# Retention, top-1 experts and a gated channel mix in one kernel: where the second half of wv is narrowed, which engine weighs the rows, and where the first constants stand

## The chip, the cores and the metric

The kernel runs on one core of one Trainium2 chip. The metric is device time in microseconds (us) of one execution; a kernel's time is the median of its runs. Engines are named as in the profile: PE is TensorE, DVE VectorE, ACT ScalarE, POOL GpSimd, SP SyncE, which issues most DMAs. PEld stands for TensorE's weight loads.

## The reference, cut to what matters

Three blocks follow one another, for 2 sequences of 768 tokens and 512 features. The weights of the third block, w_k, w_v and w_r, arrive in double precision; the rest is f32.

```python
# 1 retention, 8 heads of 64, in blocks of 64 tokens
intra = einsum(qb, kb) * Dmask @ vb
inter = (qb * lam_pow) @ kv_state
out = intra + inter
kv_state = lam_block * kv_state + einsum(kb * rev_pow, vb)
# 2 top-1 experts: one of 8 per token (a token can keep its predecessor's)
h = max(x[b, s] @ w1[e], 0)          # w1[e]: 512 x 1024
out[b, s] = p[e] * (h @ w2[e])       # w2[e]: 1024 x 512
# 3 channel mix
xk = mu_k * x + (1 - mu_k) * x_prev
xr = mu_r * x + (1 - mu_r) * x_prev
k = max(xk @ w_k, 0)                 # 512 x 1024
v = k * k @ w_v                      # 1024 x 512
r = sigmoid(xr @ w_r)                # 512 x 512
return r * v
```

## The kernel before, in words

The order of instructions on every engine is written out by hand: what the code issues first, the engine has first in its queue.

**First stage (to about 85 us).** Retention and routing in 12 units of 128 tokens (a pair of units, one per sequence, makes a chunk). `load_qk(u)` and `load_kv(u)` are SyncE's loads of 512 KB each; the two `kv` loads of a chunk fill one tile, and two such tiles exist. `iot`, which holds index patterns, takes the place of one of them until `constants()` (L244) has read it. `scores(u)` (L262) makes the product of q and k on TensorE and multiplies it with the mask on VectorE (`stm`, L281); with the second unit of a chunk it scales k for the state on ScalarE (`kd`, L267). `values(u)` (L284) makes output and state, `gate(u)` the gate's logits. `constants()` is called after the first unit's scores: four scans from `lamp` into `tab` and eight small operations on VectorE.

**Experts (about 85 to 280 us).** Each product is made of three, of high and low parts in fp32r: high x high, high x low, low x high (`split3`, L649). A weight comes in pieces of 128 x 1024 f32: `w_load` (L139) has SyncE load one into one of four `raw` buffers, `w_split` (L147) makes the high part on ScalarE (L158) and the low part on VectorE (L159), then loads the piece four further on. Per expert there are `up` (four times: eight products, then `hh` on ScalarE, L666, and `hl` on VectorE, L667), `flip` of the next expert's inputs (L646, `xsTh`, `xsTl`), and `down` for two halves of 128 tokens, whose results (`y`, L713) GpSimd scatters to `Y_n`. At four points of `up` and four of `down` the function `side_w` (L972) is called; I number its 64 calls 0 to 63, so that expert e has calls 8e to 8e + 7, the first four in `up`. In each call it divides a weight piece and takes a step of a generator:

- `narrow()` (L751), called `conv`: narrows wk, wr and the first half of wv from double precision to f32, part by part (128 x 512). A part has three steps, each with two VectorE operations (`narrow_1` L740 and L741, `narrow_2` L744 and L745, `narrow_3` L748 and L749). The third step also queues the DMA that writes the part to DRAM (`written`, issued at the next call), issues the next part's `magnitude` on ScalarE (L736), and has SyncE read the part after that into one of two `raw64` buffers. What is written is loaded again later as ordinary weight pieces, which wait for the writes. Parts 0 to 15; the last is written out at call 52.
- `direct()` (L788), called `tail`, from call 56: the four pieces of the second half of wv. Each is loaded in double precision into a `raw` buffer by `w_load`, narrowed in the same six VectorE operations, and divided at once into high and low parts (L803, L808). Two pieces fall into expert 7, two into the channel mix, between `r_part(0)` and `v_part(0)`.

w_v's high and low parts stand where those of expert 6's w2 were, so they can be written only after expert 6.

**Passage.** While expert 7 runs its `down`, the first 256 tokens are prepared for the channel mix: VectorE weighs rows that are already back from DRAM (`xg_`, L888) and the expert's own results (`weighed`, L907, `yll`); TensorE moves both into `ps_f` (`others` L902, `own` L920); `mix_first` mixes them.

**Channel mix (about 280 us to the end).** Six groups n of 256 tokens. `read(n)` fetches rows from `Y_n`, `weigh(n)` (L1026) multiplies the two halves by the gate's probability, one on VectorE (L1033), one on ScalarE (L1031); `fetch(n)` (L1038) transposes on TensorE (L1051) and copies on ScalarE (L1052); `mix(n, i)` makes the inputs of w_k (i = 0) and w_r (i = 1) on ScalarE (L941, L953) and VectorE (L945, L954). `k_part(n)` makes four steps of 24 products with `rl` and Square on ScalarE, `sq` and `k2l` on VectorE (L1105, L1106). `r_part(n)` and `v_part(n)` make the rest; VectorE multiplies both into `o` (L1134). In the steady loop the order is `v_part(n-1)`, with `weigh(n+1)`, `fetch(n+1)`, `read(n+2)` and `mix(n+1, 0)` behind its first half, then `r_part(n)`, `k_part(n+1)`, `mix(n+1, 1)`. For group 1 weighing and fetching lie in `k_part(0)` (`first_k`, L1141), behind its third and fourth step.

Of the kernel before, what the change touches and what calls it, by code (L numbers as in the profile page):

```python
# [44 lines left out]
def kernel(  # L45
# [84 lines left out]
    for kind, i, src, n, f in plan:  # L130
        m = PIECE // f
        if i == NE + 1:
            pieces += [("d", NE, wv, NF, DM, j, 1) for j in (NV, NV + 1)]
        pieces += [(kind, i, src, n, f, j, m) for j in range(0, n, m)]
    pieces += [("d", NE, wv, NF, DM, j, 1) for j in range(NV + 2, NF)]
    staged = {}
    at = [0, 0]

    def w_load():  # L139
        if at[0] < len(pieces):  # L140
            kind, i, src, n, f, j, m = pieces[at[0]]
            t = stp.tile([P, m, f], mybir.dt.int64 if kind == "d" else F32, name=f"raw{at[0]}", tag="raw")
            sp.dma_start(out=t, in_=src[:, j : j + m, :])
            staged[at[0]] = t
            at[0] += 1
# [37 lines left out]
    with ExitStack() as actx:  # L183
# [35 lines left out]
        load_kv(0)  # L219
        load_kv(1)  # L220
        sp.dma_start(out=lamp, in_=lam_p)
        sp.dma_start(out=trw[:, :, P:], in_=wg)
        sp.dma_start(out=mus, in_=mu)
        load_qk(2)

        pool.affine_select(out=tri, in_=ones, pattern=[[1, P]], compare_op=ALU.is_gt, fill=0.0, base=0, channel_multiplier=-1)
# [340 lines left out]
        for i in range(NU + 1):  # L567
# [11 lines left out]
            if i < NU - 1:  # L579
                scores(i)  # L580
                if i == 0:
                    constants()
                if i % B:
                    step()
                if i >= 2:
                    gate(i - 2)
                    if i % B:
                        routing.append(route((i - 2) // B))
                    step()
                if i >= 1:  # L590
                    values(i - 1)
                step()
            elif i == NU - 1:
                gate(i - 2)
                step()
                routing.append(route((i - 2) // B))
                step()
                scores(i, step)
                values(i - 1, {2: step, 3: step})
                step()  # L600
# [29 lines left out]
    with ExitStack() as bctx:  # L630
# [120 lines left out]
        def narrow():  # L751
# [3 lines left out]
            for src, dst in ((wk, wk32), (wr, wr32), (wv, wv32)):  # L755
                sv, dv = (x.rearrange("p a b -> p (a b)") for x in (src, dst))
                parts += [(sv[:, j : j + n], dv[:, j : j + n]) for j in range(0, dv.shape[1], n)]
            raws, ts = {}, {}

# [14 lines left out]
            for k in range(len(parts)):  # L774
# [5 lines left out]
                narrow_3(raws[k], ts[k].bitcast(F32), ts[k].bitcast(F32), t2, t2.bitcast(F32))  # L780
                written.append(lambda t=t2, k=k: sp.dma_start(out=parts[k][1], in_=t.bitcast(F32)))
                begin(k + 1)
                read(k + 2)
                yield

        spare_sb = []

        def direct():  # L788

            todo = [i for i, x in enumerate(pieces) if x[0] == "d"]  # L790
            raws, ts = {}, {}
            part = {}

            def begin(i):
                raws[i] = staged.pop(i).rearrange("p a b -> p (a b)")
                pl, bufs = (spare_sb[0], 2) if spare_sb else (tp, 1)
                ts[i] = pl.tile([P, DM], I32, name="t", tag="t", bufs=bufs)
                magnitude(raws[i], ts[i])

            def high_part(i):  # L800
                if i in part:
                    h, l, x = part[i]
                    act.copy(out=h, in_=x)  # L803

            def low_part(i):
                if i in part:
                    h, l, x = part[i]
                    dve.tensor_tensor(out=l, in0=x, in1=h.bitcast(F32), op=ALU.subtract)  # L808
                    w_load()

            last = None
            for k, i in enumerate(todo):
                while at[1] < i:
                    w_split()
                    yield
                if i not in ts:
                    begin(i)
                    yield
                raw, t = raws[i], ts[i]
                low, high = (raw.bitcast(F32).rearrange("p (n t) -> p n t", t=2)[:, :, x] for x in range(2))  # L820
                h, l = (x[:, pieces[i][5], :] for x in W["w2", NE])
                high_part(last)

                narrow_1(t)
                narrow_2(raw, t, t, high.bitcast(I32))
                if spare_sb and i + 1 in todo:
                    begin(i + 1)
                yield
                narrow_3(raw, high, low, t, high)
                at[1] += 1  # L830
                part[i] = h, l, high
                if i + 1 in todo and i + 1 not in ts:
                    begin(i + 1)
                low_part(last)
                last = i
                yield
            high_part(last)
            yield
            low_part(last)

# [128 lines left out]
        calls = [0]  # L969
        tail = direct()  # L970

        def side_w():  # L972
            c = calls[0]
            calls[0] += 1
            late = list(written)
            if c < 56:
                w_split(1 if c > 1 else 2)
            if c == 2 or c >= 4:
                next(conv, None)
            if c >= 56:  # L980
                for _ in range((1, 3, 1, 1, 2, 1, 0, 1)[c - 56]):
                    next(tail)
            for w in late:
# [17 lines left out]
    with ExitStack() as mctx:  # L1001
        mp = mctx.enter_context(tc.tile_pool(name="mp", bufs=2))
        spare_sb.append(mp)
        psr = mctx.enter_context(tc.tile_pool(name="psr", bufs=1, space=PSUM))
# [21 lines left out]
        def weigh(n):  # L1026
            if n < NN:
                for i in range(2):
                    u, x = unit(n, i), xgs[n][:, i, :]
                    if i:  # L1030
                        act.activation(out=x, in_=x, func=AF.Copy, scale=pe_p[:, u : u + 1])  # L1031
                    else:
                        dve.tensor_scalar(out=x, in0=x, scalar1=pe_p[:, u : u + 1], scalar2=None, op0=ALU.mult)  # L1033

# [74 lines left out]

        def r_part(n, xr, after):  # L1110
            sgs[n] = []
            for t in range(2):
# [6 lines left out]
                sgs[n].append(sg)  # L1119
                after(t)  # L1120

# [19 lines left out]
        def first_k(fp):  # L1141
            if fp == 0:
                mix_first(1, 1)
                x_new(1)
                for a in range(2):
                    act.copy(out=xt[1][:, 2 * a : 2 * a + 2, 0:1], in_=px[1 + a][:, :, GS - 1 : GS])
            if fp == 2:
                weigh(1)
            if fp == NF // 2 - 1:
                fetch(1)  # L1150
                xk[1] = mix(1, 0)
                read(2)

        def tail_1(t):
            for _ in range(2 * t):
                next(tail, None)

        def tail_2(_):
            next(tail, None)

# [5 lines left out]
        k_part(0, xk[0], pk, first_k)  # L1166
        r_part(0, xr[0], tail_1)
        k_part(1, xk[1], {}, tail_2)
        xr[1] = mix(1, 1)
        for _ in tail:  # L1170
            pass
        for n in range(1, NN):
# [8 lines left out]
            v_part(n - 1, ahead)  # L1181
            r_part(n, xr[n], none)
            if n + 1 < NN:
# [52 lines left out]
```

## Time and profile before

| | |
|---|---|
| median of 3 runs | 477.5 us (476.89 to 478.0) |
| profiled execution | 476.17 us, span 474.5 us |
| PE busy | 444.6 us, 94% of the span |
| PEld | 395.2 us, 83% |
| DVE | 315.6 us, 67% |
| ACT | 229.2 us, 48% |
| POOL | 63.6 us, 13% |
| mean granted clock of TensorE | 0.985 |
| DMA | 83.98 MB, mean 177 GB/s |

The span is the time from the first to the last instruction of the profiled execution; it and the time of that execution differ by what lies around it. Busy shares are means over stages with different limits: VectorE is busy throughout the experts and half idle in the channel mix. In a timeline each line begins with start and duration in us, then engine, line of the kernel, operation, output and inputs; `[2.08 <-DVE xg L1033]` says that the engine had been idle for 2.08 us and what ended it.

### The profile page before, as it was taken

The numbers are of one execution on the slowest core, as the hardware profiler recorded it, in microseconds if no ns is written. First come the engines' busy times: TensorE is split into PE (matmuls) and PEld (weight loads), VectorE is DVE, ScalarE is ACT, GpSimd is POOL, SyncE is SP. The second block draws the span as 40 slices with busy tenths as digits, with TensorE's granted clock in tenths as the row PEclk, the third lists the DMA queues.
The fourth block names the chain that finished last, engine by engine and source line by source line (L and its number), as shares of the span: only waits on it lengthen the run. The fifth ranks groups of instructions, "written<-read, shape, count | busy, mean of one in ns | idle before, by whom it ended". The sixth has DMA issues, their size and how long they took to land.

```text
span 474.5 us, 8310 instructions
## 1 busy us (share of the span) xinstructions
PE 444.6 (94%) x3243; PEld 395.2 (83%) x3243; DVE 315.6 (67%) x608; ACT 229.2 (48%) x390; POOL 63.6 (13%) x90
## 2 busy tenths in 40 slices
PE   7899988999999999999999989997989989989997
PEld 5788876889798898989898978896977968969886
DVE  4678886775989989989895777785163253551601
ACT  2455523655457556656463536754253353452410
POOL 2233324311212123212101001000000000000000
PEclk9899999999999999999999999998998999999999
DMA  7699964397969899999976533002002011000011
GB/s 253 230 350 338 362 248 135 114 317 263 342 214 379 267 360 323 336 342 338 318 231 198 188 111 112 2 1 68 22 1 88 1 51 39 0 24 22 1 45 46
DMA packets 28679, 83.98 MB, mean 177 GB/s; under 512 B 4303, under 2 KB 5083, under 8 KB 28636
## 3 DMA queue, kind: packets, MB, share of 16 engines
q1 hardware_dynamic: 24572, 72.40, 45.0%
q0 software_dynamic: 2624, 8.39, 4.8%
q10 hardware_dynamic: 1440, 2.62, 1.5%
q8 instruction: 26, 0.43, 0.4%
q14 instruction: 17, 0.14, 0.1%
HBM read 68.19 MB, written 15.21 MB: 176 GB/s over the span
## 4 chain that ended last, share of the span: by engine, by line
PE 50%; DVE 16%; DMA 6%; ACT 6%; issue 3%; DVEq 0%; SPq 0%; ACTq 0%
DMA raw<-in_wk_dram 4%; PE ps_y L654 4%; PE ps_y L652 4%; PE ps_y L653 4%; PE ps_h L654 4%; PE ps_h L653 4%; PE ps_h L652 4%; PE ps_k L1067 3%; PE ps_k L1066 3%; PE ps_v L654 3%; PE ps_v L652 3%; PE ps_k L1073 3%; PE ps_v L653 3%; PE ps_r L653 2%; PE ps_r L654 2%
## 5 line engine op out<-in xcount | busy, mean ns | idle before, releaser
L652 PE MATMUL ps_h<-xsTh,w1h 128*128 128x256 f32 x256 | 72.8, 285 | 2.0 <-DVE hl L667 2.0
L653 PE MATMUL ps_h<-xsTl,w1h 128*128 128x256 f32 x256 | 72.8, 284 | 0.2
L654 PE MATMUL ps_h<-xsTh,w1l 128*128 128x256 f32 x256 | 72.4, 283 | 0.0
L652 PE MATMUL ps_y<-w2h,hh 128*128 128x512 f32 (+1 forms) x136 | 52.6, 387 | 0.0
L654 PE MATMUL ps_y<-w2h,hl 128*128 128x512 f32 (+1 forms) x136 | 52.1, 383 | 0.2
L653 PE MATMUL ps_y<-w2l,hh 128*128 128x512 f32 (+1 forms) x136 | 51.9, 382 | 0.0
L652 PEld LDWEIGHTS ps_h<-xsTh,w1h 128*128 128x128 f32 x256 | 49.0, 191 | 3.0 <-DVE hl L667 2.4
L653 PEld LDWEIGHTS ps_h<-xsTl,w1h 128*128 128x128 f32 x256 | 49.0, 191 | 0.9 <-DVE xsTl L177 0.5
L1105 DVE TENSOR_TENSOR sq<-rl 128x512 f32<-128x512 f32 x24 | 16.5, 689 | 49.4 <-ACT rl L1102 49.4
L654 PEld LDWEIGHTS ps_h<-xsTh,w1l 128*128 128x128 f32 x256 | 49.0, 192 | 0.0
L159 DVE TENSOR_TENSOR w1l<-raw,w1h 128x1024 fp32r<-128x1024 f32 x38 | 46.0, 1216 | 1.2 <-ACT w1h L158 1.2
L159 DVE TENSOR_TENSOR w2l<-raw,w2h 128x1024 fp32r<-128x1024 f32 x34 | 41.5, 1220 | 5.7 <-ACT w2h L158 5.6
L158 ACT CAST w1h<-raw 128x1024 fp32r<-128x1024 f32 x38 | 39.2, 1053 | 6.5 <-DMA raw<-in_w_dram 6.4
L652 PE MATMUL ps_v<-w2h,k2h 128*128 128x512 f32 (+1 forms) x104 | 40.2, 387 | 0.0
L654 PE MATMUL ps_v<-w2h,k2l 128*128 128x512 f32 (+1 forms) x104 | 39.8, 382 | 0.0
L653 PE MATMUL ps_v<-w2l,k2h 128*128 128x512 f32 (+1 forms) x104 | 39.7, 381 | 0.0
L723 POOL DMA_INDIRECT Y_n<-y,sidx x16 | 18.5, 1159 | 142.6 <-ACT y L713 69.8
L158 ACT CAST w2h<-raw 128x1024 fp32r<-128x1024 f32 x34 | 35.6, 1046 | 4.1 <-DMA raw<-in_w_dram 4.1
L736 ACT ACTIVATE t<-raw 128x512 f32<-128x512 f32 x20 | 13.5, 675 | 41.4 <-DMA raw<-in_wk_dram 14.2
L654 PEld LDWEIGHTS ps_y<-w2h,hl 128*128 128x128 f32 x136 | 25.6, 188 | 6.4 <-DVE hl L667 1.1
L1102 ACT ACTIVATE rl<-ps_k 128x512 f32<-128x512 f32 x24 | 14.3, 597 | 32.8 <-PE ps_k L1073 32.8
L653 PEld LDWEIGHTS ps_y<-w2l,hh 128*128 128x128 f32 x136 | 25.6, 188 | 5.1
(213 smaller groups left out, 991.8 us busy)
## 6 DMA issues: line engine op xcount, KB each, us to landing
raw<-in_w_dram SPq DMA_DIRECT2D x64, 512.0 KB, 6.1
kv<-in_kv_dram SPq DMA_DIRECT2D x12, 512.0 KB, 7.5
qk<-in_qk_dram SPq DMA_DIRECT2D x11, 512.0 KB, 8.6
raw<-in_wk_dram SPq DMA_DIRECT2D x8, 512.0 KB, 7.9
raw<-in_wv_dram SPq DMA_DIRECT2D x8, 512.0 KB, 6.1
out_dram<-o SPq DMA_DIRECT2D x11, 256.0 KB, 2.0
X_n<-xn ACTq DMA_DIRECT2D x10, 256.0 KB, 5.8
xg<-Y_n SPq DMA_DIRECT2D x10, 256.0 KB, 2.7
```

The costliest lines, as they stand in the source:

```text
L158: act.copy(out=hi[:, j : j + m, :], in_=t)
L159: eng.tensor_tensor(out=lo[:, j : j + m, :], in0=t, in1=hi[:, j : j + m, :].bitcast(F32), op=ALU.subtract)
L652: pe.matmul(ps, wh, xh, start=first, stop=False)
L653: pe.matmul(ps, wh, xl, start=False, stop=False)
L654: pe.matmul(ps, wl, xh, start=False, stop=last)
L723: pool.indirect_dma_start(out=Y_n[:, :], out_offset=bass.IndirectOffsetOnAxis(ap=sidx[:, t, e : e + 1], axis=0), in_=y, in_offset=None)
L736: act.activation(out=t.bitcast(F32), in_=words(raw)[2], func=AF.Abs)
L1066: pe.matmul(ps[:, j, :], wkh[:, d, f], x[0][:, d, :], start=j == d == 0, stop=False, skip_group_check=True)
L1067: pe.matmul(ps[:, j, :], wkl[:, d, f], x[0][:, d, :], start=False, stop=False, skip_group_check=True)
L1073: pe.matmul(ps[:, j, :], wkh[:, d, f], x[1][:, d, :], start=False, stop=d == ND - 1, skip_group_check=True)
L1102: act.activation(out=rl, in_=ps, func=AF.Relu)
L1105: dve.tensor_tensor(out=sq, in0=rl, in1=rl, op=ALU.mult)
```

## The change

The four pieces of the second half of wv are no longer loaded by `w_load`. `narrow()` has four more parts (16 to 19), which are read into `raw64` like the others; their result is not written to DRAM but stays in its `t2` tile, and `divide()` makes high and low parts of it at calls 56, 57, 59 and 62. `direct()` and all calls of `tail` go, those in the channel mix as well. `side_w` gets a table: conversion steps are left out at calls 11 and 19, two are taken at 44, 46 and 52 to 54; w_split goes on to call 61.

`weigh` uses ScalarE for both halves; the first weighing stands behind the second step of `k_part(0)`. `constants()` is called after the scores of unit 1, and the load of unit 1's `kv` is issued behind `lamp`, the gate's weights, `mu` and the `qk` of unit 2.

```diff
@@ pieces
-        if i == NE + 1:
-            pieces += [("d", NE, wv, NF, DM, j, 1) for j in (NV, NV + 1)]
         pieces += [(kind, i, src, n, f, j, m) for j in range(0, n, m)]
-    pieces += [("d", NE, wv, NF, DM, j, 1) for j in range(NV + 2, NF)]
@@ start
         load_kv(0)
-        load_kv(1)
         sp.dma_start(out=lamp, in_=lam_p)
         sp.dma_start(out=trw[:, :, P:], in_=wg)
         sp.dma_start(out=mus, in_=mu)
         load_qk(2)
+        load_kv(1)
...
                 scores(i)
-                if i == 0:
+                if i == 1:
                     constants()
@@ narrow
+            parts += [(wv[:, j, :], j) for j in range(NV, NF)]
...
-                written.append(lambda t=t2, k=k: sp.dma_start(out=parts[k][1], in_=t.bitcast(F32)))
+                if isinstance(parts[k][1], int):
+                    whole.append((parts[k][1], t2.bitcast(F32)))
+                else:
+                    written.append(lambda t=t2, k=k: sp.dma_start(out=parts[k][1], in_=t.bitcast(F32)))
                 begin(k + 1)
                 read(k + 2)
@@ direct() goes, divide() comes
+        whole = []
+
+        def divide():
+
+            j, x = whole.pop(0)
+            hi, lo = (w[:, j, :] for w in W["w2", NE])
+            act.copy(out=hi, in_=x)
+            dve.tensor_tensor(out=lo, in0=x, in1=hi.bitcast(F32), op=ALU.subtract)
@@ side_w
-            if c < 56:
-                w_split(1 if c > 1 else 2)
-            if c == 2 or c >= 4:
-                next(conv, None)
-            if c >= 56:
-                for _ in range((1, 3, 1, 1, 2, 1, 0, 1)[c - 56]):
-                    next(tail)
+            ws, ns, vs = 1, 1, 0
+            if c < 4:
+                ws, ns = (2, 2, 1, 1)[c], c == 2
+            elif c in (11, 19):
+                ns = 0
+            elif c in (44, 46):
+                ns = 2
+            elif c >= 52:
+                ws, ns, vs = (
+                    (1, 2, 0), (1, 2, 0), (1, 2, 0), (1, 0, 0), (1, 0, 1), (1, 1, 1), (0, 2, 0), (0, 1, 1), (1, 1, 0), (1, 1, 0), (0, 0, 1), (0, 0, 0)
+                )[c - 52]
+            w_split(ws)
+            for _ in range(ns):
+                next(conv, None)
+            for _ in range(vs):
+                divide()
@@ weigh
-                    if i:
-                        act.activation(out=x, in_=x, func=AF.Copy, scale=pe_p[:, u : u + 1])
-                    else:
-                        dve.tensor_scalar(out=x, in0=x, scalar1=pe_p[:, u : u + 1], scalar2=None, op0=ALU.mult)
+                    act.activation(out=x, in_=x, func=AF.Copy, scale=pe_p[:, u : u + 1])
@@ first_k
-            if fp == 2:
+            if fp == 1:
                 weigh(1)
@@ channel mix
-        r_part(0, xr[0], tail_1)
-        k_part(1, xk[1], {}, tail_2)
+        r_part(0, xr[0])
+        k_part(1, xk[1], {}, none)
         xr[1] = mix(1, 1)
-        for _ in tail:
-            pass
```

## Rows read from the trace of the kernel before

**Rows 1.** Waits of TensorE: who for whom, us, times, longest us.
```profile
PE ps_t L1051 <- DVE xg L1033: 11.1, 5, 2.8
...
PE ps_h L652 <- DVE hl L667: 2.0, 2, 1.0
```

**Rows 2.** Timeline of TensorE: first products of four `v_part`, the fourth `fetch`.
```profile
315.33 0.40 PE L652 MATMUL ps_v<-w2h,k2h 128*128 128x512 f32 x1
...
348.65 0.40 PE L652 MATMUL ps_v<-w2h,k2h 128*128 128x512 f32 x1
...
381.32 0.40 PE L652 MATMUL ps_v<-w2h,k2h 128*128 128x512 f32 x1
...
389.03 1.09 PE L1051 MATMUL ps_t<-ident,xg 128*128 128x128 f32 x8 [2.08 <-DVE xg L1033]
389.88 0.47 PE L652 MATMUL ps_v<-w2h,k2h 128*128 128x512 f32 x1
...
412.40 0.40 PE L652 MATMUL ps_v<-w2h,k2h 128*128 128x512 f32 x1
```

**Rows 3.** Timeline of VectorE ahead of the fourth `fetch`.
```profile
387.89 0.68 DVE L1134 TENSOR_TENSOR o<-ps_v,sg 128x512 f32<-128x512 f32 x1
388.49 0.48 DVE L1033 TENSOR_SCALAR xg<-xg,pe_p 128x512 f32<-128x512 f32 x1
```

**Rows 4.** Timeline of ScalarE ahead of the fourth `fetch`.
```profile
387.16 0.72 ACT L1031 ACTIVATE xg<-xg,pe_p 128x512 f32<-128x512 f32 x1
```

**Rows 5.** Windows: stretch, busy us of PE, PEld, DVE, ACT, POOL, PEclk, DMA, GB/s.
```profile
358.00:359.00 1.00, 1.00 (x4) 0.81 (x3) 0.23 (x1) 0.91 (x3) 0.19 (x1) 0.50 0.96 371
```

**Rows 6.** Timeline of ScalarE in `k_part(0)`: the third `rl`.
```profile
294.53 0.58 ACT L1102 ACTIVATE rl<-ps_k 128x512 f32<-128x512 f32 x1
```

**Rows 7.** Timeline of TensorE: the first `fetch`.
```profile
297.42 1.07 PE L1051 MATMUL ps_t<-ident,xg 128*128 128x128 f32 x8 [2.07 <-DVE xg L1033]
```

**Rows 8.** Chain that ended last: start us, us, what; the cast in `mix(1,0)`.
```profile
302.89 0.63 ACT w1h L953
```

**Rows 9.** Timeline of TensorE in expert 7: it goes on after `yll`.
```profile
278.17 0.39 PE L920 MATMUL ps_f<-perm,yll 128*128 128x256 f32 x1 [0.42 <-DVE yll L914]
```

**Rows 10.** Timeline of VectorE: the first `hl` of expert 7.
```profile
259.09 0.69 DVE L667 SCALAR_TENSOR_TENSOR hl<-ps_h,hh 128x512 fp32r<-128x512 f32 x1 [5.16 <-ACT hh L666]
```

**Rows 11.** Waits of SyncE's queue, 234 to 263 us.
```profile
SPq L143 <- DMA wv<-t: 4.1, 1, 4.1
```

**Rows 12.** Timeline of SyncE: the load of wv's last f32 piece.
```profile
255.08 0.32 SPq L143 DMA_DIRECT2D raw<-wv  x1
```

**Rows 13.** DMA issues, 255.4 to 258 us: count, KB each, median us to landing.
```profile
raw<-in_wv_dram SPq DMA_DIRECT2D x2, 512.0 KB, 6.0
```

**Rows 14.** Windows, columns as in rows 5: from the first `hl` of expert 7 to `yll`.
```profile
259.09:278.11 19.02, 17.05 (x117) 15.37 (x115) 16.32 (x26) 8.53 (x12) 1.08 (x1) 1.00 0.58 194
```

**Rows 15.** Groups of VectorE: shapes, count | busy us, mean ns | idle before.
```profile
L159 DVE TENSOR_TENSOR w2l<-raw,w2h 128x1024 fp32r<-128x1024 f32 x34 | 41.5, 1220 | 5.7 <-ACT w2h L158 5.6
...
L808 DVE TENSOR_TENSOR w2l<-raw,w2h 128x512 fp32r<-128x512 f32 x4 | 2.7, 685 | 0.0
```

**Rows 16.** Timeline of ScalarE ahead of the first `hh` of expert 2.
```profile
143.25 0.68 ACT L736 ACTIVATE t<-raw 128x512 f32<-128x512 f32 x1 [3.83 <-DMA raw<-in_wk_dram]
```

**Rows 17.** Timeline of TensorE: the last quarter of expert 2's `up`.
```profile
145.67 0.39 PE L652 MATMUL ps_h<-xsTh,w1h 128*128 128x256 f32 x1 [1.02 <-DVE hl L667]
```

**Rows 18.** Timeline of VectorE at the start: the scans of `constants`.
```profile
11.35 1.37 DVE L246 TENSOR_TENSOR_SCAN tab<-lamp,zer 128x128 f32<-128x128 f32 x4 [3.38 <-DMA lamp<-in_lam_p_dram]
```

**Rows 19.** Timeline of TensorE at the start: fourteen of unit 2's scores.
```profile
16.29 2.06 PE L276 MATMUL st<-qk 64*128 64x128 f32 x14 [1.91 <-DVE stm L281]
```

**Rows 20.** Timeline of ScalarE at the start: the scaled k of chunk 0.
```profile
11.14 2.44 ACT L267 ACTIVATE kd<-kv,rev 128x128 f32<-128x128 f32 x8 [8.13 <-DMA kv<-in_kv_dram]
```

**Rows 21.** SyncE's issue of units 2 and 3's `qk`, and time to landing.
```profile
6.22 1.35 SPq L207 DMA_DIRECT2D qk<-in_qk_dram  x2
...
qk<-in_qk_dram SPq DMA_DIRECT2D x2, 512.0 KB, 6.8
```

More of the change, by code (lines that the diff above doesn't have):

```diff
@@ L141, in w_load @@
             kind, i, src, n, f, j, m = pieces[at[0]]
-            t = stp.tile([P, m, f], mybir.dt.int64 if kind == "d" else F32, name=f"raw{at[0]}", tag="raw")
+            t = stp.tile([P, m, f], F32, name=f"raw{at[0]}", tag="raw")
             sp.dma_start(out=t, in_=src[:, j : j + m, :])
@@ L784, in narrow @@
                 yield
[L786 to L839, printed above, removed]
+        whole = []
[4 more added lines that the diff above has]
+            dve.tensor_tensor(out=lo, in0=x, in1=hi.bitcast(F32), op=ALU.subtract)
         conv = narrow()
@@ L969 @@
         calls = [0]
-        tail = direct()
         def side_w():
@@ L1002 @@
         mp = mctx.enter_context(tc.tile_pool(name="mp", bufs=2))
-        spare_sb.append(mp)
         psr = mctx.enter_context(tc.tile_pool(name="psr", bufs=1, space=PSUM))
@@ L1108, in k_part, with r_part @@
                 after(fp)
-        def r_part(n, xr, after):
+        def r_part(n, xr):
             sgs[n] = []
@@ L1119, in r_part @@
                 sgs[n].append(sg)
-                after(t)
         def v_part(n, after):
@@ L1152, in first_k @@
                 read(2)
[L1154 to L1159, printed above, removed]
         xk, xr = {0: x0[0]}, {}
@@ L1181 @@
             v_part(n - 1, ahead)
-            r_part(n, xr[n], none)
+            r_part(n, xr[n])
             if n + 1 < NN:
```

## The prediction

> **What bounds the kernel now.** I read the waits of TensorE first, then timelines of each engine around the longest of them, then SyncE's waits and the DMA issues where the change moves transfers. From expert 1 on TensorE is all but always busy, so time is lost where it waits, and the first view says where: 11.1 us in five waits for the weighing on VectorE (L1033), the longest 2.8, and 2.0 us in two waits for `hl` (L667) [rows 1]. All five stand in the channel mix, each ahead of a `fetch`. The fourth is typical: TensorE has finished the first half of `v_part`, VectorE finishes a mix, multiplies `o`, and only then weighs (388.49 to 388.97); the transposes start at 389.03 after 2.08 us of idleness [rows 2, 3]. ScalarE had weighed the other half already at 387.16 [rows 4]. So the order on VectorE ends that wait, not data and not ScalarE.
>
> From one `v_part` to the next takes 33.32, 32.67 and 31.08 us (starts at 315.33, 348.65, 381.32, 412.40) [rows 2]. The wait inside the first is the 2.8, inside the others 2.08; the rest of the difference is the granted clock, 0.50 for some time after the first two waits and not after the third [rows 5].
>
> **The change part by part.**
>
> *Weighing on ScalarE alone.* It removes a VectorE multiplication of 0.48 us per pair of units and adds a ScalarE activation of 0.72 [rows 3, 4]. In the steady part ScalarE has nothing between its last mix cast and the weighing, so the first half is weighed 387.16 to 387.88, the second to 388.5 (two in a row overlap by 0.1, as VectorE's pair in rows 3). The transposes of the first half go at 387.94, those of the second at 388.56; eight took 0.85 (389.03 to 389.88) [rows 2], four take 0.43, and `v_part` goes on at 388.99 instead of 389.88: -0.9. Four such waits: -3.6 (each between -0.5 and -1.0).
>
> The Trainium skill speaks against this: "ScalarE: Activation LUTs", section "Rules for kernel authors", wants a plain multiplication on VectorE. The trace agrees on the price, 0.72 against 0.48, and by price alone the four fetches would cost 4 x 0.24 = +1.0 instead of -3.6; which engine is free earlier decides here by rows 3 and 4. That rule is rival D.
>
> *The first weighing also moves up, from behind the third step of `k_part(0)` to behind the second.* ScalarE would take it at 294.53, where it now starts the third `rl` [rows 6], and end near 295.9. TensorE then transposes from 295.4 to 296.4 instead of from 297.42 after 2.07 us of idleness [rows 7]: 1.8 earlier. What is late next: the third and fourth `rl` and Square slip into time in which ScalarE waited for those transposes, so the copies out of PSUM stay where they are, the second high part of `mix(1,0)` still ends at 303.5 [rows 8], and `k_part(1)`, now due at 301.9, waits some 0.7 after its first eight products. I take -1.1 (0 to -1.9).
>
> *The tail of direct narrowing leaves the channel mix.* Fifteen VectorE operations go from between `r_part(0)` and `v_part(0)`. What they cost TensorE is the first long wait, 2.8 instead of 2.08: -0.7 (0 to -0.8).
>
> *Clock.* The stretches at 0.50 cost 33.32 - 31.08 - 0.7 = 1.5 and 32.67 - 31.08 = 1.6 us. The waits before them shrink to about 1.2. The trace has 0.50 after idleness of 2.8 and after one of 2.08, and none after the 2.08 of rows 2 and the 2.07 of rows 7. I take both away: -3.1 (0 to -3.1).
>
> *wv's second half through the common narrowing.* Calls 52 to 54 (expert 6, down) now narrow parts 16 and 17, twelve VectorE operations; calls 57 to 61 narrow 18 and 19 in place of the two direct pieces; calls 56, 57 and 59 each divide a piece ahead of the `yll` that TensorE waits for until 278.17 [rows 9]. VectorE is free for 5.16 us ahead of the first `hl` of expert 7 [rows 10], which would hide much of parts 16 and 17, were it not for the order of the transfers. SyncE's load of wv's last f32 piece waits 4.1 us for the write of part 15 and is issued at 255.08 [rows 11, 12]. In the new order the read of part 18 (call 53) stands behind it and goes out at 255.45, in the place of the two direct pieces, which took 6.0 us to land [rows 13]: 261.1 or so. The `magnitude` of part 18 is issued in call 54, and behind it on ScalarE stand the cast of call 55, `y` of expert 6, the first `hh` of expert 7 and all casts after. So VectorE gets its split of call 55 only 1.6 us after the landing (`magnitude` and cast), at 262.7. From there to the end of `yll` it has: what it did from 259.09 to 278.11, 16.32 us busy [rows 14], one split of 1.22 more, two divisions of 0.69 more [rows 15], less 0.1 of overlap in each: 18.8. It ends at 281.5 instead of 278.1: **+3.4**. TensorE meets this as waits of up to 2 us each for the last `hl`, for `xg` and for `yll`; its next wait is that of rows 7, so nothing gives the time back. Bounds: no wait of ScalarE, VectorE busy without a gap: -0.3; a landing after 6.8 us, as in rows 21: +4.2. The casts of the divisions lie in ScalarE's free time (8.53 busy of 19.02) [rows 14]; the fourth division, call 62, follows `yll`: 0, or 0.69 if TensorE waits for it.
>
> Two conversion steps are left out at calls 11 and 19 and made up at 44 and 46. Where ScalarE waits 3.83 us for a read until 143.25, ahead of the first `hh` of expert 2, the `magnitude` is now issued one call later, behind that `hh`; TensorE's wait of 1.02 at 145.67 shrinks [rows 16, 17]. VectorE too has one step less to do by then; I take -0.8 (0 to -1.0). The other wait for `hl` comes in call 8, ahead of the first omission, and stays. The steps made up lie in expert 5, where TensorE waits for nothing: 0.
>
> *The start.* `constants` now stands behind the second unit's scores. Before, VectorE waited 3.38 us for `lamp`, and TensorE later 1.91 for `stm` behind it [rows 18, 19]. That goes. But `kv` of unit 1 moves behind `lamp`, `wg`, `mu` and the `qk` of unit 2 on SyncE, and `kd` on ScalarE started at 11.14 because that `kv` landed then [rows 20]. As the fifth large transfer it lands like that `qk` now, 6.8 us after an issue at 6.2 [rows 21]: 13.0, 1.9 later. TensorE had two scores of unit 2 done at 16.29 - 1.91 = 14.38; it now has them at 16.2 and goes on without a wait. That alone is -0.1; with a landing 0.4 earlier, as nothing large is ahead of it that is not there now, -0.5, which I take. Ends: +0.7 (landing 0.7 later) and -1.5 (landing 1.4 earlier). `iot` comes free no later, so the `kv` loads behind it on SyncE are not held up.
>
> The sum: -3.6 - 1.1 - 0.7 - 3.1 + 3.4 - 0.8 - 0.5 = **-6.4 us**. The profiled execution took 476.17 (span 474.5), so 469.8; the median of the runs lies 1.3 above that execution, and the forecast for a median is 477.5 - 6.4 = **471.1**.
>
> **Rivals.**
> A, the forecast: 0.50, from 468.5 to 473.5.
> B, the added narrowing is hidden: part 18 lands before ScalarE comes to it, +3.4 becomes -0.3, 467.4. For it: the free 5.16 us. Against it: the issue behind 255.08. 0.25.
> C, the slower side, TensorE's clock. Place: the three waits that I put into expert 7 within 17 us. Price: 1.5 of half clock for each, as after the waits in rows 5, 4.6 together; idleness of that kind then also brings the falls in the channel mix back, 3.1. -6.4 + 4.6 + 3.1 = +1.3: 478.8. It decides from the point at which idleness of 1 to 2 us is enough for a fall. Against it: 2.08 and 2.07 without one. 0.09.
> D, ScalarE's price decides, the weighing ending as late as VectorE's did: +1.0 for -3.6, and the clock falls stay: -6.4 + 4.6 + 3.1 = +1.3, 478.8. Against it: rows 4. 0.04. This is what the rule of the Trainium skill, "ScalarE: Activation LUTs", would make of it.
> E, the early parts do nothing, because a transfer takes the place of the wait removed (`kv` at the start, a read at expert 2): -5.1, 472.4. 0.12.
>
> The numbers: the range 465.5 to 475.5 holds A, B and E but for their ends; C and D lie outside. All bounds at their good ends give 465. A measurement of this kernel tells about 0.2%, 1 us. Faster by more than that: A, B and E less a little, 0.85; within it 0.05; slower 0.10, C and D less a little.
>
> **What would show it.** In the changed profile TensorE should wait 1.0 to 1.3 us for ScalarE's weighing at each of four fetches, and hardly at the first; the granted clock should be 1.00 through the channel mix, and `v_part` to `v_part` 30.2 us. ScalarE should wait for a read of wv shortly before the first `hh` of expert 7, and TensorE for `hl`, `xg` and `yll` there. At the start the wait for `stm` should be gone and `kd` begin near 13. I am wrong in size if that ScalarE wait is missing, and wrong in sign if the clock falls in expert 7.

## The result, and the profile after

The changed kernel takes 472.32 us (median; 470.58 to 473.34), the kernel before 477.75 beside it (476.89 to 480.09): ratio 0.9875, 95% interval 0.9828 to 0.9922, so -5.4 us where -6.4 was forecast. The two profiled executions, on which the working rests, are 476.17 and 471.87 us (spans 474.5 and 470.2): -4.3.

First the waits of TensorE after (who for whom: us, times, longest us), to hold against [rows 1].

```profile
PE ps_t L1011 <- ACT xg L993: 3.9, 4, 1.0
PE ps_h L649 <- DVE hl L664: 2.4, 2, 2.1
PE pk L313 <- ACT kd L264: 2.2, 1, 2.2
PE st L273 <- DMA qk<-in_qk_dram: 1.9, 1, 1.9
...
PE ps_f L875 <- DVE yll L869: 1.8, 1, 1.8
PE ps_f L857 <- DVE xg__3370 L843: 1.5, 1, 1.5
```

The five waits for the weighing, 11.1 us, are four of 1.0; the first `fetch` waits for nothing. In expert 7 TensorE now waits 2.12 us for `hl` and 1.75 for `yll`, which was 0.42 before [rows 9]. The wait for `xg`, 1.50, is not new: the kernel before has it too.

```profile
275.98 0.94 PE L902 MATMUL ps_f<-ident,xg__3343 128*128 128x128 f32 x4 [1.54 <-DVE xg__3343 L888]
```

The timelines of expert 7 show how the waits come about: SyncE's (the load of wv's last f32 piece, then the read of part 18), ScalarE's (the `magnitude` of part 18), VectorE's (the split behind it) and TensorE's, all of the changed kernel.

```profile
253.65 0.32 SPq L140 DMA_DIRECT2D raw<-wv  x1
254.02 0.44 SPq L761 DMA_DIRECT2D raw<-in_wv_dram  x1
```
```profile
260.49 0.69 ACT L733 ACTIVATE t<-raw 128x512 f32<-128x512 f32 x1 [7.49 <-DMA raw<-in_wv_dram]
```
```profile
262.14 1.23 DVE L156 TENSOR_TENSOR w1l<-raw,w1h 128x1024 fp32r<-128x1024 f32 x1 [4.25 <-ACT w1h L155]
```
```profile
264.02 0.39 PE L649 MATMUL ps_h<-xsTh,w1h 128*128 128x256 f32 x1 [2.12 <-DVE hl L664]
...
277.52 0.94 PE L857 MATMUL ps_f<-ident,xg__3370 128*128 128x128 f32 x4 [1.50 <-DVE xg__3370 L843]
...
281.03 0.39 PE L875 MATMUL ps_f<-perm,yll 128*128 128x256 f32 x1 [1.75 <-DVE yll L869]
...
299.68 1.27 PE L1011 MATMUL ps_t<-ident,xg 128*128 128x128 f32 x8
...
318.55 0.40 PE L649 MATMUL ps_v<-w2h,k2h 128*128 128x512 f32 x1
...
325.17 1.27 PE L1011 MATMUL ps_t<-ident,xg 128*128 128x128 f32 x8 [0.98 <-ACT xg L993]
326.19 0.47 PE L649 MATMUL ps_v<-w2h,k2h 128*128 128x512 f32 x1
...
348.71 0.40 PE L649 MATMUL ps_v<-w2h,k2h 128*128 128x512 f32 x1
```

This is the mechanism that the prediction put there: a read that goes out behind the last load of wv (at 254.02), seven and a half microseconds in which ScalarE stands, VectorE 4.25 us idle behind it and then never again before `yll`. The windows of the changed kernel (columns as in [rows 5]) show the clock: it falls to its lower level twice in expert 7, after the waits of 2.12 and of 1.50 and 1.75 us, and no more in the channel mix.

```profile
264.00:266.00 2.00, 1.98 (x12) 1.98 (x13) 1.95 (x3) 2.00 (x5) 0.21 (x1) 0.70 0.69 168
266.00:268.00 2.00, 2.00 (x11) 2.00 (x11) 1.97 (x4) 1.56 (x3) 0.00 (x0) 0.50 0.61 234
...
282.00:284.00 2.00, 2.00 (x12) 2.00 (x11) 0.50 (x2) 0.85 (x2) 0.00 (x0) 0.50 0.00 0
284.00:286.00 2.00, 2.00 (x14) 2.00 (x14) 0.54 (x2) 0.00 (x0) 0.00 (x0) 0.68 0.00 0
...
384.00:386.00 2.00, 1.02 (x7) 0.50 (x5) 1.32 (x3) 1.81 (x3) 0.00 (x0) 1.00 0.00 0
```

Cut at the same instructions of TensorE (expert 7's first `ps_h`, its `yll` product, the first products of the five `v_part`), the 4.3 us are:

| stretch | before | after | difference | forecast |
|---|---|---|---|---|
| start to expert 7's `up` | 255.40 | 253.12 | -2.28 | -1.3 |
| expert 7's `up` to `yll` | 22.77 | 27.91 | **+5.14** | +3.4 |
| `yll` to the first `v_part` | 37.16 | 37.52 | **+0.36** | -1.1 |
| first to second `v_part` | 33.32 | 30.16 | -3.16 | -3.1 |
| second to third | 32.67 | 30.16 | -2.51 | -2.5 |
| third to fourth, fourth to fifth | 31.08 each | 30.16 each | -1.84 | -1.8 |

The forecast for the channel mix is right to a tenth. What is off lies in expert 7 and just behind it, and, with the opposite sign, ahead of expert 7.

### The profile page after: what moved, and what is told of

Read it like the earlier page. It is cut to its first block, busy times and chain, and to the rows that moved or that the text cites. A ratio compares the mean times of both kernels' runs of the same rounds, so it can differ in the third digit from the quotient of the medians.

```text
span 470.2 us, 8303 instructions
## 1 busy us (share of the span) xinstructions
PE 444.7 (95%) x3243; PEld 395.4 (84%) x3243; DVE 311.9 (66%) x603; ACT 231.8 (49%) x395; POOL 67.3 (14%) x90
## 4 chain that ended last, share of the span: by engine, by line
PE 42%; DVE 17%; DMA 11%; ACT 7%; issue 4%; SPq 0%; DVEq 0%; ACTq 0%
PE ps_k L1026 4%; PE ps_k L1027 4%; PE ps_k L1033 4%; DMA raw<-in_w_dram 4%; PE ps_v L649 3%; PE ps_v L651 3%; PE ps_v L650 3%; DMA raw<-in_wk_dram 3%; DVE w1l L156 3%; DMA raw<-in_wv_dram 3%; DVE w2l L156 3%; PE ps_y L651 2%; PE ps_y L650 2%; PE ps_y L649 2%; PE ps_r L649 2%
## 5 line engine op out<-in xcount | busy, mean ns | idle before, releaser
L720 POOL DMA_INDIRECT Y_n<-y,sidx x16 | 20.9, 1308 | 143.2 <-ACT y L710 83.1
```

The costliest lines, as they stand in the source:

```text
L720: pool.indirect_dma_start(out=Y_n[:, :], out_offset=bass.IndirectOffsetOnAxis(ap=sidx[:, t, e : e + 1], axis=0), in_=y, in_offset=None)
```

## The experiments

The kernel before had a median of 478.86, 478.67 and 478.06 us beside the first four, the next four and the last two. One kernel's executions differ by 1% and more (the changed kernel 470.13 to 474.78 us in one set of six), so a difference of 1 us between two kernels is at the edge of what these counts tell apart.

**One part of the change alone (x_weigh).** The kernel before with
```diff
-                    if i:
-                        act.activation(out=x, in_=x, func=AF.Copy, scale=pe_p[:, u : u + 1])
-                    else:
-                        dve.tensor_scalar(out=x, in0=x, scalar1=pe_p[:, u : u + 1], ...)
+                    act.activation(out=x, in_=x, func=AF.Copy, scale=pe_p[:, u : u + 1])
...
-            if fp == 2:
+            if fp == 1:
```


> The kernel before with ScalarE weighing both halves, the first weighing one step earlier, and nothing else of the change. Theory (the order on VectorE ended the waits): the four later waits at fetch fall from 2.1 to 2.8 us to about 1.0, the first one goes; 4 to 5 us less, and up to 3 us more if the granted clock no longer falls in the channel mix: 470 to 474 where the kernel before has 477.7. Rival (a plain multiplication belongs on VectorE, 0.72 against 0.48 us): 1 us more, 478.7.

471.77 us (470.85 to 473.29), ratio 0.9841 [0.9803, 0.9879]: this one edit is worth as much as the whole change. Its waits of TensorE for the weighing:
```profile
PE ps_t L1048 <- ACT xg L1030: 6.1, 4, 3.2
```
Three of 1.0, and a first one of 3.2 where the changed kernel has 0.98 at 325.17: the tail of direct narrowing still stands there on VectorE, and the clock falls after it. From the first `v_part` to the second takes 33.97 us, against 30.16 without the tail: moving the tail away is worth 3.8 us once ScalarE weighs. From expert 7's `up` to the first `v_part` x_weigh takes 60.23 us, the changed kernel 65.43. So in these two profiles the wv part gains 3.8 and costs 5.2.

**The start alone (x_start).** The kernel before with `load_kv(1)` and `constants` moved:
```diff
-        load_kv(1)
...
         load_qk(2)
+        load_kv(1)
...
-                if i == 0:
+                if i == 1:
```


> The kernel before with only the two edits of the start: constants behind the second unit's scores, kv of unit 1 issued later. Theory: TensorE's wait for stm goes and a wait for kd comes in its place, because kv lands 2 us later; 0.3 to 1.3 us less, 476.4 to 477.4. Rival (the wait for VectorE simply goes): 1.9 us less, 475.8.

475.36 us (474.24 to 476.72), ratio 0.992 [0.989, 0.995], -3.5 us: more than either had it, though the span of its profile is only 1.4 shorter. That profile begins expert 7 2.36 us earlier than the one before (253.04 for 255.40) and loses 0.94 of it from `yll` to the first `v_part` (38.10 for 37.16), where its clock falls to 0.50. The wait for `stm` is gone and one of 1.8 for `kd` has come. What the start is worth is taken up at x_kv1.

**The wv part alone (x_wv).** The kernel before with the change's `narrow`, `divide`, `side_w` and without the tail; weighing and start as before.


> The kernel before with only wv's second half through the common narrowing and the table of side_w; weighing and start as before. Theory: 3 to 4 us more before yll in expert 7, 0.8 less in expert 2, 0.7 to 2 less in the channel mix, where the tail is gone: 477 to 479.5, against 477.7. Rival (the added narrowing is hidden): 474 to 476.

483.12 us (477.08 to 484.56), ratio 1.0091 [1.0064, 1.0119]: slower, and by more than the theory had. Its profile is of its fastest run, 477.08; the other nine took 480.89 to 484.56, and no profile shows what makes them longer. In the one profile the largest new wait of TensorE stands in expert 7:
```profile
PE ps_h L649 <- DVE hl L664: 3.6, 1, 3.6
```
From expert 7's `up` to the first `v_part` it takes 66.56 us against 59.93 before. In the channel mix, where only the tail is gone, the first long wait is 2.08 instead of 2.81, and the first two stretches from `v_part` to `v_part` take 32.66 and 31.06 us for 33.32 and 32.67.

The medians of the three parts nearly add up: -7.1 for the weighing, -3.5 for the start, +4.3 for wv make -6.3, and the whole change measured -5.4 here and -6.7 in x_again below.

**The next read one call later (x_late18).** The changed kernel with the `magnitude` of part 18 in call 56 instead of 54, behind the first `hh` of expert 7:
```diff
-                    (1, 2, 0), (1, 2, 0), (1, 2, 0), (1, 0, 0), (1, 0, 1), (1, 1, 1), ...
+                    (1, 2, 0), (1, 2, 0), (1, 1, 0), (1, 0, 0), (1, 1, 1), (1, 1, 1), ...
```


> The changed kernel with one conversion step (the third of part 17, which issues the magnitude of part 18) taken in call 56 instead of call 54. Theory (ScalarE was held by the read of part 18): the wait of 7.5 us on ScalarE ahead of the first hh of expert 7 shrinks to about 1, the wait for yll ends 3 to 4.5 us earlier, about 468, against 472.3 for the changed kernel. Rival (the amount of VectorE work ahead of yll decides, whatever holds ScalarE): the same work, 472.

471.61 us (469.92 to 473.45), ratio 0.9837 [0.9793, 0.9881]: no gain that can be told. ScalarE's stand shrinks from 7.49 to 4.01 us and TensorE's wait of 2.12 goes, but the waits of TensorE further on are these:
```profile
272.11 0.50 PE L651 MATMUL ps_y<-w2h,hl 128*128 128x512 f32 x1 [1.46 <-DVE hl L664]
...
276.85 0.94 PE L857 MATMUL ps_f<-ident,xg__3370 128*128 128x128 f32 x4 [1.76 <-DVE xg__3370 L843]
...
280.36 0.58 PE L875 MATMUL ps_f<-perm,yll 128*128 128x256 f32 x1 [1.24 <-DVE yll L869]
```
`yll` comes at 280.36 instead of 281.03, and the clock is 0.50 from 278 to 284. Part 18 itself landed later in this profile, ScalarE going on with it at 263.06 instead of 260.49. My theory, that the standing read alone made the 5.1, fell; the rival, the amount of VectorE's work ahead of `yll`, was left.

**Work taken from ahead of `yll` (x_again, x_spread).** x_again is the changed kernel. x_spread adds to x_late18 that the last two splits of wr and the divisions of parts 18 and 19 go to calls 62 and 63, behind `yll`. The division of call 62 stood behind `yll` already, so what leaves the stretch ahead of it is two splits and one division, about 2.9 us of VectorE (2 x 1.14 + 0.60) and not the 3.5 of the expectation:
```diff
-                    ..., (0, 2, 0), (0, 1, 1), (1, 1, 0), (1, 1, 0), (0, 0, 1), (0, 0, 0)
+                    ..., (0, 2, 0), (0, 1, 0), (0, 1, 0), (0, 1, 0), (1, 0, 1), (1, 0, 1)
```


> The changed kernel itself, once more, as the yardstick for the other three on the same chip. 471 to 473.5 us, ratio to the kernel before 0.984 to 0.991; in its trace ScalarE again stands about 7 us before the magnitude of part 18 and the y product of the last expert starts 27 to 28 us after its first up product.

471.99 us (470.13 to 474.78), ratio 0.9877 [0.9846, 0.9907]. From expert 7's `up` to `yll` its profile takes 29.16 us, over a microsecond more than expected.

> The changed kernel with the magnitude of part 18 one call later (as in x_late18) and with both splits of the receptance weights' last two pieces and the divisions of parts 18 and 19 behind the last expert's gathered y (calls 62 and 63 in place of 59 to 61): the same operations, about 3.5 us of VectorE (2 x 1.14 + 2 x 0.60) taken from ahead of yll. Theory (the amount of VectorE work ahead of yll, and the clock that falls when TensorE stands, make the added narrowing cost 5.1 us in place of 3.4): yll 274.5 to 276.5, no stretch at 0.50 in the last expert, 464.5 to 467.5 us, ratio 0.971 to 0.979. Rival 1 (the read of the next part is what holds the last expert, so only the later magnitude counts): as x_late18, 470.5 to 472.5 us. Rival 2 (what is moved comes back as a late receptance weight or a late division in the channel mix): TensorE waits there for w1l, w2l or rl grow by 2 to 3.5 us and the time stays at 469 to 472 us.

468.13 us (466.42 to 470.20), ratio 0.9776 [0.9748, 0.9805]; the intervals of the two don't touch. The time is 0.6 above the theory's range. TensorE's waits there in x_spread:
```profile
273.05 0.50 PE L651 MATMUL ps_y<-w2h,hl 128*128 128x512 f32 x1 [1.46 <-DVE hl L664]
...
278.21 0.39 PE L875 MATMUL ps_f<-perm,yll 128*128 128x256 f32 x1 [0.62 <-DVE yll L869]
...
282.08 0.38 PE L875 MATMUL ps_f<-perm,yll 128*128 128x256 f32 x1 [1.35 <-DVE t L892]
```
Expert 7's `up` to `yll` takes 23.15 us (22.77 before) and the granted clock is 1.00 all through it. `yll` itself stands at 278.21 and not at 276, because expert 7 began at 255.06; by the stretch the theory holds. Rival 2 is out in the channel mix, where every stretch takes 30.14 to 30.16 us as in the changed kernel. But right behind `yll` the moved work does cost something: VectorE is busy with it until 281.6, and TensorE waits 1.35 us at 282.08, which the changed kernel does not.

**Only that move (x_move).** As x_spread, but with the `magnitude` of part 18 early again.


> The changed kernel with only the second half of the spreading: the splits of the receptance weights' last two pieces and the divisions of parts 18 and 19 behind the last expert's gathered y (about 3.5 us of VectorE taken from ahead of yll), and the magnitude of part 18 early, as in the changed kernel, so that ScalarE stands for its read and VectorE stands 4.2 us behind it. Theory (VectorE's work and its idle time both stand ahead of yll, and either alone can be borne): from the last expert's first up product to yll 23.5 to 25.5 us, between x_spread's 23.2 and the changed kernel's 27.9 to 29.2, and 468.5 to 470.5 us. Rival 1 (the amount of work alone decides): 23 us and the time of x_spread, 468.1 within 0.7 us. Rival 2 (TensorE's own stand at 262 to 264 us, which the early magnitude makes, drops the clock again whatever comes later): a stretch at 0.50 from 264 us, 26 to 28 us, and 470.5 to 472.5 us.

470.59 us (468.63 to 472.34), ratio 0.9841 [0.9799, 0.9883]; `up` to `yll` 25.62 us. Its waits at the two ends of expert 7 and the clock behind the first:
```profile
267.03 0.58 PE L649 MATMUL ps_h<-xsTh,w1h 128*128 128x256 f32 x1 [2.92 <-DVE hl L664]
...
280.95 0.39 PE L875 MATMUL ps_f<-perm,yll 128*128 128x256 f32 x1 [0.62 <-DVE yll L869]
```
```profile
268.00:270.00 2.00, 2.00 (x12) 2.00 (x11) 2.00 (x4) 2.00 (x5) 0.00 (x0) 0.50 0.90 272
```
Rival 2's fall of the clock came, from 267 on; the time lies a tenth above the theory's range, inside rival 2's. Alone, neither x_late18 nor x_move can be told from the changed kernel.

The stretches from `up` to `yll`, 27.9 us in the changed kernel, 26.3 in x_late18, 25.6 in x_move and 23.2 in x_spread, can't be set against one another as they are, since part 18 landed at different times. In all of these profiles ScalarE stands until it has landed, and so the moment at which it goes on shows the landing, as here in x_move and x_spread:
```profile
263.51 0.68 ACT L733 ACTIVATE t<-raw 128x512 f32<-128x512 f32 x1 [7.09 <-DMA raw<-in_wv_dram]
```
```profile
264.00 0.67 ACT L733 ACTIVATE t<-raw 128x512 f32<-128x512 f32 x1 [4.28 <-DMA raw<-in_wv_dram]
```
From there to `yll`:

| expert 7 | landing | `yll` | us between |
|---|---|---|---|
| as changed (changed kernel, x_again, x_kv1, x_noskip, x_wv) | 260.28 to 261.08 | 280.64 to 281.60 | 20.3 to 20.5 |
| `magnitude` later (x_late18) | 263.06 | 280.36 | 17.3 |
| work moved (x_move) | 263.51 | 280.95 | 17.4 |
| both (x_spread) | 264.00 | 278.21 | 14.2 |
| both (x_both, below) | 258.98 | 273.19 | 14.2 |

So both count, by 3.1 to 3.2 us each, and they add up. In x_late18 and x_move a landing 2.0 and 2.4 us later than in any profile of the first row took most of the gain away again; with one profile of each, whether the edit or the execution made it later stays open. x_both landed earliest of all with the same expert 7 as x_spread, so the landing can move by 5 us without an edit there.

**The skipped steps (x_noskip).** The changed kernel without
```diff
-            elif c in (11, 19):
-                ns = 0
-            elif c in (44, 46):
-                ns = 2
```


> The changed kernel with a narrowing step at every call again in place of none at calls 11 and 19 and two at 44 and 46. Theory (the skipped steps give 0.8 us where SP's late write held the read behind it in the third expert): expert 2's first down product 0.5 to 1.0 us later than the changed kernel's 146.4 us, the time 0.5 to 1.0 us longer, 472.5 to 473.5 us. Rival (the 1.0 us of the third expert's lead is the start's, carried on): the first down product of expert 2 within 0.3 us of 146.4, the time within 0.4 us of the changed kernel.

473.69 us (471.13 to 475.81), ratio 0.9901 [0.9872, 0.9931], 1.7 above x_again with intervals that overlap. Its trace has the wait of [rows 17] back:
```profile
144.94 0.39 PE L649 MATMUL ps_h<-xsTh,w1h 128*128 128x256 f32 x1 [1.15 <-DVE hl L664]
```
and x_again has instead, in the same expert's `down`:
```profile
150.63 0.50 PE L651 MATMUL ps_y<-w2h,hl 128*128 128x512 f32 x1 [0.80 <-DVE hl L664]
```
So the skips take one wait away and bring two thirds of it back a little later. By the whole of expert 2, from its first product to that of expert 3, they save 0.7 us: 25.29 without them, 24.59 and 24.63 with them (changed kernel, x_again). The rest of the 1.7 us is not explained.

**The start once more (x_both, x_kv1).** x_both is x_spread, x_kv1 the changed kernel, both with `load_kv(1)` at its old place, and the constants still behind the second unit's scores:
```diff
         load_kv(0)
+        load_kv(1)
...
         load_qk(2)
-        load_kv(1)
```


> x_spread with the second unit's keys and values loaded at their old place, ahead of the waiting list at the start; the constants stay behind the second unit's scores. Theory (the wait of ScalarE for kv at the start, 10.4 us against 8.1, costs TensorE 2.2 us once and the constants' new place gives 2.6 back): the wait of pk for kd falls from 2.2 to under 0.5 us and the time is 1 to 2 us under x_spread, 463 to 466 us. Rival (the second unit's keys and values were not what came late, the loads behind them then come later by the same amount): the first transposed val at 26.0 to 26.5 us as before, and the time within 0.7 us of x_spread.

466.30 us (464.22 to 467.44), ratio 0.9741 [0.9723, 0.9760], 12.4 us under the kernel before and under both kernels of the diff by more than their intervals: the best version of these, 0.3 above the theory's range. The wait of `pk` for `kd` is 0.4.

> The changed kernel with only the second unit's keys and values loaded at their old place; the constants stay behind the second unit's scores, and the last expert is as in the changed kernel. Theory (their new place makes the first unit's keys and values land later and costs TensorE 2.2 to 3.7 us at pk, of which the wait for qk that varies between runs hides some): the wait of pk for kd under 0.6 us, the first transposed val 1 to 2 us earlier than in the changed kernel's two profiles (26.07 and 24.75), 470 to 471.3 us. Rival (the 1.8 us between x_both and x_spread come from elsewhere): the time within 0.7 us of the changed kernel's 472.

472.67 us (469.20 to 473.24), ratio 0.9877 [0.9833, 0.9920]: no gain, as the rival had it; the wait for `kd` is 0.9. Whether the order of the loads is worth anything stays open. The profiles lean to it: the first transposed `val`, the end of the start, comes at 24.75 to 26.54 in seven profiles with both of the change's edits there, at 24.01 and 25.42 with the old load order, at 26.41 to 27.23 in three with the old start. The landing of the first `qk` loads makes TensorE wait between 0.0 and 2.2 us in all from one profile to the next (x_again, x_both), and that is as large as what is looked for.

## Why the prediction was right in sign and short in size

**Weighing, tail and clock of the channel mix: right.** Four fetches came to 30.16 us a unit, -0.92 each, both falls of the clock are gone, -3.1 and -2.5 for the first two stretches. ScalarE takes its 0.72 and TensorE still waits half as long as before, 0.98 for 2.08: position in the queue decides, not price, and rival D (the rule of the Trainium skill, "ScalarE: Activation LUTs", section "Rules for kernel authors", to multiply on VectorE) is out: x_weigh, the edit against the rule by itself, is 1.6% faster. The tail's -0.7 is right where VectorE still weighs (2.81 to 2.08 in x_wv). What I had not seen is that it is worth 3.8 us once ScalarE weighs: before, VectorE's weighing hid most of it.

**wv's narrowing in expert 7: the mechanism right, the landing too early.** On the clock on the wall `yll` stands 2.86 us later than before; the forecast was -1.3 + 3.4 = +2.1. Step by step: the read went out at 254.02, 1.43 earlier than worked out (255.45), which is the lead of -1.3 that the sum counts on. From its issue to ScalarE going on with it took 6.47 us (260.49), where the working has 5.65. The split came 1.65 later (1.6), and the end of `yll` another 18.83 later, at 280.97 (18.8). So the term that was mis-sized is the landing of part 18, by 0.8. The working also has two slips that nearly cancel: by its own rows 255.45 + 6.0 is 261.45 and not 261.1, and its sum for VectorE is 18.6 and not 18.8.

The +5.14 of the table is larger than these 2.86 because it also holds the 2.28 by which TensorE began expert 7 earlier. Its end hangs on the chain of transfers (write of part 15, load, read of part 18, then `magnitude`, split and VectorE without a gap) and not on TensorE. Five profiles with this same expert 7 show it (changed kernel, x_again, x_kv1, x_noskip, x_wv): TensorE begins it at 253.12, 251.64, 252.47, 254.68 and 251.98, and `yll` comes at 281.03, 280.80, 281.60, 280.64 and 281.37. Three microseconds of lead of TensorE are worth nothing at its end. SyncE's queue spreads less: it issues the write of part 15 within 1.6 us (248.13 to 249.73), the load behind that write goes out 4.27 to 5.20 us later, longest where the write was earliest (5.20 in x_again and x_wv), and so the reads of part 18 stand within 1.1 us (253.71 to 254.82). What makes that write longer was not tried. The first fall of the clock, at 264 to 268, costs next to nothing of its own, since TensorE waits again at 277.52: x_noskip has no fall there and x_again a longer one, and from the landing to `yll` they take 20.3 and 20.5 us. So the sentence that I would be wrong in sign if the clock falls in expert 7 did not hold: it fell twice, and the sign stayed.

**The first weighing, -1.1, measured +0.36: the clock took it.** This is the larger miss, 1.5 us. The wait of [rows 7] is gone (299.68, none), and `k_part(1)` waits 0.5 (0.7 was forecast). But behind `yll` TensorE ran at half clock from 282 to past 284. x_again, whose `yll` waited as long, did not have that fall and took 36.01 us for the stretch: -1.15. So the term was right, and a price of the size that rival C names was paid once. It is not the wv part's, though: x_weigh and x_start, with expert 7 as before, have the same fall there. C is also wrong in that such falls bring back those in the channel mix. The 0.8 and the 1.5 are about what the profiled executions fall short of the forecast, -4.3 for -6.4. That the profile shows the fall in the changed kernel and not in the kernel before is luck of the two executions, as the last section shows.

**The early parts: -2.28 for -1.3.** Of it 0.34 lies ahead of the first `val` (0.5 forecast), 1.00 in the stretch from there to the fourth, 0.9 behind it. Expert 2, with the skips, takes 24.59 us for 25.15, -0.56 (0.8 forecast); expert 1 takes 24.57 for 25.23, because the wait for `hl` of which the prediction says that it stays, 1.00, shrank to 0.33. It is 0.57 in x_noskip, so the skips are not all of the reason, and the rest is not known. The 1.00 is not the change's: x_wv, with the old start, has it too, and x_late18, with the new one, has not (32.99 and 34.02 us from the first to the fourth `val`, 34.00 before and 33.00 after). It is told in the last section. Without it the profile would fall short of the forecast by another 1.0 us, so that the two came as near as they did is in part luck. Rival E (they do nothing) is out by x_start, but its profile does not account for all that its times gained.

**What the change is worth, then:** weighing alone 1.6%, wv and the start together nothing on top of it as they are placed, and 4 us more once two splits, one division and one `magnitude` stand behind what TensorE waits for.

## What to carry to other kernels

Before adding gains ahead of a place to a cost at that place, ask what sets the end there: if it is a chain of transfers and a full queue, only a lead of that chain counts, and one of the engine that waits is lost. Work that is moved from a place where an engine is waited for should be counted against the slack up to the next thing that is waited for, operation by operation; here 2.9 us of it, put behind that point, together with one read waited for later, decided between nothing and 4 us. And a term read from a wait that two causes share shows only the one that ends last: the tail seemed to cost 0.7 us until the weighing beside it was gone.

## What the hardware showed that I had not expected

Idleness of the same length lowered TensorE's clock in one execution and not in another. The plainest pair is x_weigh and the kernel before, whose expert 7 is the same: both wait 1.54 us for `xg` and 0.43 and 0.42 for `yll`, and right behind it the first has 0.50 and the second 1.00 (columns as in [rows 5]):
```profile
278.00:280.00 2.00, 2.00 (x11) 2.00 (x11) 0.23 (x1) 1.00 (x2) 0.00 (x0) 0.50 0.30 123
```
```profile
278.00:280.00 2.00, 1.83 (x15) 1.83 (x16) 0.42 (x2) 1.04 (x2) 0.00 (x0) 1.00 0.56 213
```
Behind `yll` the clock also fell in the changed kernel (waits of 1.50 and 1.75 us) and in x_kv1 (1.49 and 1.75), not in x_again (0.42 and 1.75), x_spread (0.62 and 1.35) or x_move (0.62 and 1.36); x_start had a fall to 0.50 behind a wait of 1.54, the kernel before none behind the 2.07 of [rows 7]. Behind the first stage, seven waits of these profiles are longer than 2.8 us (2.81 to 3.59: kernel before, x_start, x_move, x_weigh, x_kv1, x_again, x_wv), and each is followed by a stretch at 0.50.

A small VectorE operation can take 1 us longer beside one of GpSimd. The same pair on VectorE and the `qd` product on GpSimd, in the kernel before and in the changed one:
```profile
58.39 1.42 DVE L467 SCALAR_TENSOR_TENSOR t<-lg,mx,idr 128x8 f32<-128x8 f32 x2
...
58.52 1.27 POOL L270 TENSOR_TENSOR qd<-qk,tab 128x512 f32<-128x512 f32 x1 [3.49 <-DMA qk<-in_qk_dram]
```
```profile
58.05 0.37 DVE L464 SCALAR_TENSOR_TENSOR t<-lg,mx,idr 128x8 f32<-128x8 f32 x2
...
59.11 1.27 POOL L267 TENSOR_TENSOR qd<-qk,tab 128x512 f32<-128x512 f32 x1 [4.43 <-PE pk L313]
```
Where `qd` ran, the pair took 1.42 us and ended with it; where it came later, 0.37. TensorE's wait for `val` behind it is the 1.00 us of the start. Other profiles show the same: `qd` starts within 0.03 us of the pair in x_noskip, which takes 1.46, and of the operation on `val` behind the pair in x_late18, which takes 1.30 in place of 0.22; each ends with `qd` or just behind it. No run tested it by itself. The Trainium skill, "SBUF — State Buffer", section "Who interferes with whom", has a VectorE instruction with two inputs in SBUF contend with a GpSimd instruction that reads SBUF, through a read interface that they share; these two rows agree with it.
